# Pooled attention and a cosine router on one core: output columns in token order, stores of 128 contiguous rows, gates of the last rows by VectorE, a schedule with other step lengths

## The chip, the cores and the metric

The kernel runs on one core of a Trainium2 chip. The metric is the device time of one execution in microseconds; the time before is the median of three runs. Everything is computed in one launch.

## The reference

```python
def _attn_ref(q, k, v):                 # 8 batches, 8 heads, 576 tokens, 64 wide
    k_p = k.reshape(B, H, Sp, pool, D).mean(axis=3)      # pool = 8, Sp = 72
    v_p = v.reshape(B, H, Sp, pool, D).mean(axis=3)
    scores = scale * np.matmul(q, k_p.transpose(0, 1, 3, 2))
    attn = softmax(scores)
    return np.matmul(attn, v_p)
...
def _moe_ref(x, expert_emb, tau, w1, w2):   # x: 4608 tokens x 512, 8 experts, F = 1024
    logits = xn @ en.T / tau            # xn, en: rows of x and expert_emb, normalized
    expert_idx = np.argmax(logits, axis=1)
    gate_w = probs[np.arange(N), expert_idx]   # probs: softmax of logits
    for e in range(E):
        mask = expert_idx == e
        h = np.maximum(x[mask] @ w1[e], 0.0)
        out[mask] = gate_w[mask, None] * (h @ w2[e])
    return out
```

The rows of x are the attention's output, heads side by side, so a batch is 576 consecutive rows of the output, each of 512 floats (2 KB).

## The kernel before

The eight batches are worked through one after the other, and attention of batch b+1 stands among the expert products of batch b. All tokens of a batch are taken to go to one expert, chosen from the mean of its pooled v; a loop at the end (line 727 on) repairs batches where other experts are needed, and is left at once where there are none.

**Loads.** GpSimd's queue loads K, V and Q of a batch (576 KB each as fp16, cast on the way from float) and the chosen expert's weights W1 and W2 (1 MB each as fp16). A round for batch b is the list `PK, W1(b), K(b+1), Q(b+1), W2(b), V(b+2)` (line 229 on); `PK` (`pick`, line 266) reads the expert's number, which VectorE finds in `choose` (line 363) from the folded V of the same batch. So a round cannot be issued before that step.

**Attention.** VectorE halves K and V by adding (`halve`, line 300, and the folds, lines 304 and 312), transposes Q in blocks (`qT`, line 385) and copies the transposed K (`kpT`, line 402). Q is loaded with 18 consecutive tokens on each of 32 partitions a head (R = 32, T = 18). TensorE makes scores in two halves (`SC`, line 415), ScalarE the exponentials (`EX`, line 428), TensorE the products with V (`PV`, line 443), VectorE divides (line 453), TensorE transposes to `xt_all`, which has the 576 tokens of a batch as columns. In the kernel before, a column is t * 32 + p for the token p * 18 + t.

**Router.** Lines 489 to 531 make the gate of every token: `gate` (line 524) leaves it in `gm_all`, 128 rows by 5 chunks. The fifth chunk holds only 64 new tokens, in its rows 64 to 127. `NE` (line 539) copies their gates to rows 0 to 63 of `gl_all` by a DMA on SyncE's queue.

**Expert products.** `H` (eight steps, line 548) multiplies W1 with `xt_all`; `HE` (lines 557, 559) is the relu, on ScalarE or VectorE; `Y` (four steps, line 563) multiplies with W2 for 128 tokens each, `YE` (lines 575, 577) scales by the gate, `ST` (line 622) stores 256 KB. The last 64 tokens are one step `YL` (line 569), with the left half of the columns in rows 0 to 63 and the right half in rows 64 to 127. `YF` scales the left half on VectorE with `gl_all` (line 577, 64x256), `YG` the right half on ScalarE with `gm_all` (line 575, 64x256), and `SL` (`put_last`, line 644) stores the two halves, 64 KB each. All stores are issued on SyncE's queue. `Y` tiles come from a ring of six, PSUM tiles from a ring of four; a tile that `YL` wrote is free again when `YF` and `YG` have run.

**Order.** `Plan` lists every step with its engine, a length in us, a priority, and what it needs. `order` (line 76) goes through a clock of its own and always takes the step that can begin first; instructions of an engine stand in the program in that order, and an engine runs them in that order. So a length changes the places of steps, not the work.

Of the kernel before, what the change touches and what calls it, by code (L numbers as in the profile page):

```python
# [16 lines left out]
ALU = mybir.AluOpType  # L17
# [38 lines left out]
class Plan:  # L56
# [5 lines left out]
    def add(self, name, engines, busy, prio, run, after=(), takes=(), uses=(), late=0.0,  # L62
            mode=None):
        if isinstance(engines, str):
            engines = (engines,)
        if not isinstance(busy, tuple):
            busy = (busy,) * len(engines)
        s = Step(name, engines, busy, late, prio, [a for a in after if a], list(takes),
                 list(uses), run, mode)
        for b in s.takes + s.uses:  # L70
            b.left += 1
        self.steps.append(s)
        self.by_name[name] = s
        return name
# [68 lines left out]
def kernel(  # L143
# [83 lines left out]
    add = plan.add  # L227
# [44 lines left out]
    def attention(b, base):  # L272
        P = PERIOD
        kr, vr, qq = Buf(kr_r), Buf(vr_r), Buf(qq_r)
        qT, kp, kpT, vp = Buf(qT_r), Buf(kp_r), Buf(kpT_r), Buf(vp_r)
        n = lambda s, *i: s + str(b) + "".join(f".{j}" for j in i)

        def pr(f):
            return base + f * P
# [3 lines left out]
        if b == 0:  # L283
            for i in range(NQ):
                add(n("Q", i), 'POOL', 0.8, at_load(n("Q", i)), lambda i=i: load_q(b, qq, i, 1),
                    takes=[] if i else [qq], uses=[qq] if i else [], mode=1.43, late=0.9)
        else:
            add(n("Q", 0), 'POOL', 0.8, at_load(n("Q", 0)), lambda: load_q(b, qq, 0, NQ),
                takes=[qq], mode=2.85, late=0.9)
# [35 lines left out]
        if b == 0:  # L325
            pv_, pk_ = Buf(psum), Buf(psum)
            add(n("KA"), 'PE', 1.75, pr(-0.5), lambda: sums(kr, pk_), [n("K"), "PRE"],
                takes=[pk_], uses=[kr], late=0.22)
            add(n("KB"), 'ACT', 0.55, pr(-0.5), lambda: [nc.scalar.copy(
                out=kp_rows()[:, a],  # L330
                in_=by_group(pk_.tile[0:G, 0:512].rearrange("g (h d) -> g h d", d=D))[:, a])
                for a in range(NQ)], [n("KA")], takes=[kp], uses=[pk_], late=0.12)
            add(n("VA"), 'PE', 1.75, pr(-0.45), lambda: sums(vr, pv_), [n("V"), "PRE"],
                takes=[pv_], uses=[vr], late=0.22)
            add(n("VB"), 'DVE', 0.6, pr(-0.45), lambda: nc.vector.tensor_copy(
                out=vp_rows(), in_=pv_.tile[0:G, 0:512].rearrange("g (a c) -> g a c", a=HP)),
                [n("VA")], takes=[vp], uses=[pv_], late=0.12)
        else:
            add(n("VA"), 'DVE', 1.14, pr(-0.5), lambda: halve(vr.tile, 4), [n("V")], uses=[vr],
                late=0.1)  # L340
            add(n("VB"), 'DVE', 0.95, pr(-0.5), v_fold, [n("VA")], takes=[vp], uses=[vr],
                late=0.1)
            add(n("KA"), 'DVE', 1.14, pr(-0.2), lambda: halve(kr.tile, 4), [n("K")], uses=[kr],
                late=0.1)
            add(n("KB"), 'DVE', 1.0, pr(-0.2), k_fold, [n("KA")], takes=[kp], uses=[kr],
                late=0.1)


        pg = Buf(psum)
# [18 lines left out]
        def onehot():  # L368
# [5 lines left out]
        add(n("GC"), 'DVE', 0.1, pr(-0.5), lambda: nc.vector.tensor_copy(  # L374
            out=mv.tile, in_=pg.tile[:, 0:4]), [n("GM")], takes=[mv], uses=[pg], late=0.1)
        add(n("GL"), 'PE', 0.13, pr(-0.5), guess, [n("GC")], uses=[pg, mv], late=0.22)
        add(n("GD"), 'DVE', 0.35, pr(-0.5), choose, [n("GL")], uses=[pg], late=0.1)
        add(n("GE"), 'DVE', 0.2, pr(0.5), onehot, [n("GD")], late=0.1)


        for a in range(NQ):
            for i in range(2):
# [10 lines left out]
        def kt():  # L393
# [5 lines left out]
                        identity=ident_h[0:G, 0:G])  # L399

        add(n("KT"), 'PE', 0.14, pr(0.0), kt, [n("KB"), "PRE"], takes=[pk], uses=[kp], late=0.22)
        add(n("KE"), 'DVE', 0.25, pr(0.0), lambda: nc.vector.tensor_copy(  # L402
            out=kpT.tile.rearrange("p a c g -> p (a c g)"),
            in_=pk.tile.bitcast(FP16)[:, 0:2 * NQ * G]), [n("KT")], takes=[kpT], uses=[pk],
            late=0.1)

        at = [Buf(at_r) for _ in range(HP)]
        for half in range(2):
            for a in range(NQ):
                pair = [Buf(psum), Buf(psum)]  # L410

                def score(a=a, half=half, pair=pair):
                    for c in range(2):
                        for m in range(QG):
                            nc.tensor.matmul(  # L415
                                out=pair[m // 2].tile[0:G, m % 2 * 512:m % 2 * 512 + HALF],
                                lhsT=kpT.tile[ts(m, R), a, c, :],
                                rhs=qT.tile[ts(m, R), a, ts(half, T // 2), c, :],
                                start=(c == 0), stop=(c == 1))

                f = 0.02 + 0.2 * half + 0.1 * a
                add(n("SC", half, a), 'PE', 0.35, pr(f), score,
                    [n("KE"), n("QT", a, half)], takes=pair, uses=[qT, kpT], late=0.22,
                    mode='r32')
                for i in range(2):
                    t = at[2 * a + i]
                    add(n("EX", half, 2 * a + i), 'ACT', 0.56, pr(f),
                        lambda t=t, p=pair[i], half=half: nc.scalar.activation(  # L428
                            out=t.tile[:, :, ts(half, HALF)],
                            in_=p.tile[0:G].rearrange("g (r c) -> g r c", r=2)[:, :, 0:HALF],  # L430
                            func=AF.Exp, scale=escale),
                        [n("SC", half, a)], takes=[] if half else [t],
                        uses=[pair[i]] + ([t] if half else []), late=0.12)


        for c in range(NC):
            px, r, x, pt = Buf(psum), Buf(r_r), Buf(x_r), Buf(psum)
# [33 lines left out]
            def square(c=c, x=x):  # L471
# [3 lines left out]
            f = 0.5 + 0.08 * c  # L475
            add(n("PV", c), 'PE', 0.27, pr(f), pv,
                [n("EX", i, j) for i in range(1 if c < 2 else 2) for j in range(HP)] + [n("VB")],
                takes=[px], uses=at + [vp], late=0.22)
            add(n("XM", c), 'DVE', 0.84, pr(f), norm, [n("PV", c)], takes=[r, x], uses=[px],
                late=0.12)  # L480
            add(n("XT", c), 'PE', 0.23, pr(f), xtr, [n("XM", c)], takes=[pt], uses=[x], late=0.22)
            add(n("XE", c), 'DVE', 0.34 if c < 4 else 0.22, pr(f), xcopy, [n("XT", c)], uses=[pt],
                late=0.1)
# [15 lines left out]
        def pick_max():  # L499
# [8 lines left out]
            late=0.22)  # L508
# [15 lines left out]
        def gate():  # L524
            nc.vector.tensor_reduce(out=z, in_=lg, axis=AX.X, op=ALU.add)
            nc.vector.tensor_tensor(out=lg, in0=oh_all[:, b],
                                    in1=eb_all[:, b].unsqueeze(1).to_broadcast([128, NC, E]),
                                    op=ALU.mult)
            nc.vector.reciprocal(out=gate_all[:, b], in_=z)
            nc.vector.tensor_reduce(out=gm_all[:, b], in_=lg, axis=AX.X, op=ALU.add)  # L530
            nc.vector.tensor_tensor(out=gm_all[:, b], in0=gm_all[:, b], in1=gate_all[:, b],
                                    op=ALU.mult)

        add(n("NA"), 'POOL', 1.25, pr(1.3), root, [n("SQ", c) for c in range(NC)], late=0.1)
        add(n("NB"), 'DVE', 0.4, pr(1.3), scaled, [n("NA"), n("RE")], late=0.1)
        add(n("NC"), 'ACT', 0.25, pr(1.3), lambda: nc.scalar.activation(
            out=lg, in_=lg, func=AF.Exp, bias=lnxs), [n("NB")], late=0.1)
        add(n("ND"), 'DVE', 0.65, pr(1.35), gate, [n("NC"), n("GE")], late=0.1)
        add(n("NE"), 'SP', 0.1, pr(1.35), lambda: nc.sync.dma_start(
            out=gl_all[0:64, b:b + 1], in_=gm_all[64:128, b, 4:5]), [n("ND")], mode=0.1, late=1.0)  # L540

# [33 lines left out]
            nc.vector.tensor_scalar(out=dst, in0=src, scalar1=g, scalar2=None, op0=ALU.mult)  # L577

    def chunk_rows(o_b, c):
        return o_b.rearrange("(p t) d -> t p d", t=T)[4 * c:4 * c + 4]  # L580

    def last_rows(o_b):
        return o_b.rearrange("(p t) (r d) -> r t p d", t=T, r=2)[:, 16:18]

    def ffn(b, base):
        n = lambda s, *i: s + str(b) + "".join(f".{j}" for j in i)
# [43 lines left out]
        def last(r):  # L630
            rows = ts(r, 64)
            scale_rows(y.tile[rows, 0:DH], p.tile[rows, r * 512:r * 512 + DH],
                       g[rows, 4:5] if r else gl_all[:, b:b + 1], 'ACT' if r else 'DVE')

        add(n("YF"), 'DVE', 0.35, f - 2.0, lambda: last(0), [n("YL"), n("NE")], takes=[y],
            uses=[p], late=0.12)
        add(n("YG"), 'ACT', 0.38, f - 2.0, lambda: last(1), [n("YL"), n("ND")], uses=[p, y],
            late=0.12)
# [88 lines left out]
    with tc.For_i(0, n_val, 1) as i:  # L727
        f_val = nc.values_load(ext_i[0:1, ds(i, 1)], min_val=0, max_val=1)
        with tc.If(f_val > 0):
# [19 lines left out]
                h_mm(xt_c, w1, w, psum.tiles[w % 4])  # L749
                h_relu(psum.tiles[w % 4], hT[w], 'ACT' if w % 2 else 'DVE')  # L750
            gl = gl_all[:, B:B + 1]
            nc.sync.dma_start(out=gl, in_=gmx[64:128, 4:5])
            y, o = y_r.tiles[0], y_r.tiles[1]
            for c in range(5):
                p = psum.tiles[c % 4]
# [56 lines left out]
```

## Time and profile before

| | us |
|---|---|
| median of 3 runs | 284.74 (284.48 to 286.25) |
| the profiled execution's own time | 285.62 |
| its span, first to last instruction | 284.0 |
| TensorE busy with products | 205.8 |
| VectorE busy | 144.5 |
| ScalarE busy | 119.4 |
| GpSimd busy | 43.9 |

The profile shows one execution. Its span is shorter than its own time by what lies before the first and behind the last instruction. Busy times overlap each other. PE is TensorE, PEld its weight loads, DVE VectorE, ACT ScalarE, POOL GpSimd and SP SyncE; a q behind a name means its instruction queue, which issues DMAs. L548 is line 548 of the kernel before. A number in brackets behind a row is the idle time of the engine just before it and what ended it. A DMA share is the mean busy share of the core's sixteen DMA engines; packet times can overlap, so it can exceed 1.

### The profile page before, as it was taken

What the parts mean: (1) busy time and instruction counts of PE and PEld (TensorE: products, weight loads), DVE (VectorE), ACT (ScalarE), POOL (GpSimd) and SP (SyncE); (2) the same over time, 40 slices, a digit from 0 to 9 for tenths busy, and PEclk for the clock granted to TensorE, in tenths of its full rate; (3) what the DMA queues carried; (4) which work ended last, traced back from release to release, by engine and by line L of the source; (5) the groups of instructions that cost most, each with busy time, mean ns of one, the idle gap of its engine ahead of it and who ended that gap; (6) DMA issues with size and microseconds to landing.
All of it is one profiled execution on the core that took longest, in us unless ns stands there. A gap on an engine that the chain in (4) does not pass through costs nothing.

```text
span 284.0 us, 5224 instructions
## 1 busy us (share of the span) xinstructions
PE 205.8 (72%) x2006; PEld 128.9 (45%) x2007; DVE 144.5 (51%) x398; ACT 119.4 (42%) x239; POOL 43.9 (15%) x59
## 2 busy tenths in 40 slices
PE   2898798868995597938995698904997069899600
PEld 1566664544563353624563354602555036476300
DVE  2178677945791557724792458514495043550200
ACT  2046285374457153453447254620542056454400
POOL 7052400700160005100060004100021000010000
PEclk9999999997999599896999599975899658999955
DMA  5979999999999937995299937992149421121120
GB/s 70 196 122 202 206 208 208 222 227 227 194 184 230 180 76 140 222 216 115 67 173 221 187 79 139 212 203 81 60 82 217 96 88 48 38 82 51 47 103 21
DMA packets 29147, 40.76 MB, mean 144 GB/s; under 512 B 4536, under 2 KB 14776, under 8 KB 29120
## 3 DMA queue, kind: packets, MB, share of 16 engines
q0 software_dynamic: 23184, 30.95, 62.5%
q1 hardware_dynamic: 5936, 9.46, 10.0%
q8 instruction: 16, 0.26, 0.4%
q14 instruction: 11, 0.09, 0.1%
HBM read 61.88 MB, written 9.44 MB: 251 GB/s over the span
## 4 chain that ended last, share of the span: by engine, by line
DMA 64%; PE 21%; DVE 4%; issue 3%; POOL 1%; ACT 1%; POOLq 1%; DVEq 0%
DMA vr<-in_v_dram 27%; DMA kr<-in_k_dram 19%; DMA gl_all<-gm_all 18%; PE pa L548 11%; PE pa L563 6%; PE pa L415 2%; DVE y L577 2%; PE pa L569 1%; POOL w L256 1%; DVE vr L301 1%; PE pa L322 1%; DVE xt_all L466 0%; ACT hT L557 0%; DVE kr L301 0%; POOLq L267 0%
## 5 line engine op out<-in xcount | busy, mean ns | idle before, releaser
L548 PE MATMUL pa<-xt_all,w 128*128 128x288 f16 x512 | 80.2, 313 | 33.4 <-DVE y L577 31.2
L548 PEld LDWEIGHTS <-w 128*128 128x128 f16 x512 | 51.3, 105 | 56.8 <-issue 41.6
L563 PE MATMUL pa<-w,hT 128*128 128x512 f16 x256 | 60.8, 383 | 4.9 <-DVE y L577 2.4
L428 ACT ACTIVATE at<-pa 72x576 f16<-72x576 f32 x64 | 37.4, 641 | 35.2 <-PE pa L415 35.1
L557 ACT ACTIVATE hT<-pa 128x576 f16<-128x576 f32 x49 | 31.8, 650 | 37.0 <-PE pa L548 35.0
L563 PEld LDWEIGHTS <-hT 128*128 128x128 f16 x256 | 24.6, 98 | 30.9 <-issue 7.3
L575 ACT ACTIVATE y<-pa,gm_all 128x512 f32<-128x512 f32 (+1 forms) x32 | 20.0, 630 | 39.9 <-PE pa L563 25.5
L472 ACT ACTIVATE sq<-x 128x512 f16<-128x512 f16 x40 | 25.1, 628 | 22.8 <-DVE x L453 18.8
L256 POOL DMA_DIRECT2D w<-in_moe_w_dram x8 | 6.4, 804 | 152.9 <-PE pa L563 120.2
L301 DVE TENSOR_TENSOR vr<-vr 72x2048 f16<-72x2048 f16 (+1 forms) x14 | 13.4, 954 | 32.8 <-DMA vr<-in_v_dram 32.6
L453 DVE TENSOR_TENSOR x<-pa,r 128x512 f16<-128x512 f32 x40 | 27.7, 691 | 1.7
L415 PE MATMUL pa<-qT,kpT 32*72 32x288 f16 x256 | 16.5, 341 | 11.4 <-DVE ssq_all L520 11.2
L385 DVE STREAM_TRANSPOSE qT<-qq 128x576 f16<-128x576 f16 x32 | 23.3, 756 | 1.5 <-DMA qq<-in_q_dram 1.5
L559 DVE TENSOR_SCALAR hT<-pa 128x576 f16<-128x576 f32 x15 | 11.4, 757 | 24.7 <-PE pa L548 24.4
L516 POOL TENSOR_TENSOR ssq_all<-ssq_all,half_c 128x5 f32<-128x5 f32 x8 | 9.9, 1242 | 51.1 <-ACT sq L472 51.1
L577 DVE TENSOR_SCALAR y<-pa,gl_all 64x256 f32<-64x256 f32 x8 | 3.8, 473 | 27.4 <-DMA gl_all<-gm_all 14.3
L466 DVE COPY xt_all<-pa 128x512 f16<-128x512 f16 (+1 forms) x40 | 14.8, 383 | 2.5 <-PE pa L461 2.4
L461 PE MATMUL pa<-ident_h,x 128*128 128x128 f16 x160 | 14.4, 224 | 2.2 <-DVE x L453 2.0
L301 DVE TENSOR_TENSOR kr<-kr 72x2048 f16<-72x2048 f16 (+1 forms) x14 | 13.3, 947 | 5.2 <-DMA kr<-in_k_dram 5.1
L415 PEld LDWEIGHTS <-kpT 32*72 32x72 f16 x256 | 5.5, 118 | 21.0 <-DVE kpT L402 11.6
L461 PEld LDWEIGHTS <-x 128*128 128x128 f16 x160 | 11.0, 100 | 8.8 <-DVE x L453 3.6
L443 PE MATMUL pa<-vpx,at 72*128 72x65 f16 x320 | 14.5, 194 | 0.0
(87 smaller groups left out, 174.6 us busy)
## 6 DMA issues: line engine op xcount, KB each, us to landing
w<-in_moe_w_dram POOLq DMA_DIRECT2D x16, 1024.0 KB, 24.2
out_dram<-y SPq DMA_DIRECT2D x32, 256.0 KB
vr<-in_v_dram POOLq DMA_DIRECT2D x8, 576.0 KB, 35.3
kr<-in_k_dram POOLq DMA_DIRECT2D x8, 576.0 KB, 25.7
qq<-in_q_dram POOLq DMA_DIRECT2D x7, 576.0 KB, 32.0
out_dram<-y SPq DMA_DIRECT2D x16, 64.0 KB
qq<-in_q_dram POOLq DMA_DIRECT2D x2, 288.0 KB, 10.1
gl_all<-gm_all SPq DMA_DIRECT2D x8, 0.2 KB
```

The costliest lines, as they stand in the source:

```text
L301: nc.vector.tensor_tensor(out=t[:, :, 0:m], in0=t[:, :, 0:m], in1=t[:, :, m:2 * m], op=ALU.add)
L385: nc.vector.transpose(out=qT.tile[:, a].rearrange("p t c e -> p (t c e)")[:, cols], in_=qq.tile[:, a, cols]),
L415: nc.tensor.matmul(out=pair[m // 2].tile[0:G, m % 2 * 512:m % 2 * 512 + HALF], lhsT=kpT.tile[ts(m, R), a, c, :], rhs=qT.tile[ts(m, R), a, ...
L428: lambda t=t, p=pair[i], half=half: nc.scalar.activation(out=t.tile[:, :, ts(half, HALF)], in_=p.tile[0:G].rearrange("g (r c) -> g r c", r ...
L453: nc.vector.tensor_tensor(out=x.tile, in0=pxv[:, :, 1:129].rearrange("p a (r d) -> p a r d", d=D), in1=r.tile.rearrange("p (a r) -> p a r" ...
L461: nc.tensor.transpose(out=pt.tile.bitcast(FP16)[:, ts(w, 128)], in_=xf[:, ts(w, 128)], identity=ident_h)
L466: nc.vector.tensor_copy(out=xt_all[:, b, :, c * 128:c * 128 + 128 - o], in_=pt.tile.bitcast(FP16)[:, 0:512].rearrange("p (w t) -> p w t", ...
L472: nc.scalar.activation(out=sq, in_=x.tile.rearrange("p a r d -> p (a r d)"), func=AF.Square, accum_out=ssq_all[:, b, c:c + 1])
L548: nc.tensor.matmul(out=p[:, half * 512:half * 512 + HALF], lhsT=w1v[:, kk, w // 2, w % 2, :], rhs=xt[:, kk, ts(half, HALF)], start=(kk == ...
L557: nc.scalar.activation(out=dst, in_=src, func=AF.Relu)
L563: nc.tensor.matmul(out=p, lhsT=hT[w][:, ts(c, 128)], rhs=w2[:, w // 2, w % 2, :], start=(w == 0), stop=(w == 7))
L575: nc.scalar.activation(out=dst, in_=src, func=AF.Copy, scale=g)
```

## The change

Five things are edited.

The columns of `xt_all` become tokens in their natural order. A score half is now 16 of the 32 partitions' worth of tokens (columns t, p with 16 values of p) instead of 9 values of t, so the first half needs both transposes; the exponential reads its PSUM tile with the t and p extents exchanged, and writes token order.

With that, a chunk of 128 columns is 128 consecutive rows of the output, and `chunk_rows` and `last_rows` no longer pick rows 18 apart. The gates of the last 64 rows are multiplied a second time on VectorE, straight to rows 0 to 63 of `gl_all`, and the DMA step `NE` is gone; `YF` needs `ND` instead. Eight step lengths of the plan are other numbers. In the repair loop a DMA becomes a VectorE copy.

```diff
-            add(n("VB"), 'DVE', 0.95, pr(-0.5), v_fold, [n("VA")], takes=[vp], uses=[vr],
+            add(n("VB"), 'DVE', 1.0, pr(-0.5), v_fold, [n("VA")], takes=[vp], uses=[vr],
...
-                                rhs=qT.tile[ts(m, R), a, ts(half, T // 2), c, :],
+                                rhs=qT.tile[ts(m, R), a, :, c, ts(half, R // 2)],
...
-                add(n("SC", half, a), 'PE', 0.35, pr(f), score,
-                    [n("KE"), n("QT", a, half)], takes=pair, uses=[qT, kpT], late=0.22,
+                add(n("SC", half, a), 'PE', 0.27, pr(f), score,
+                    [n("KE"), n("QT", a, 0), n("QT", a, 1)], takes=pair, uses=[qT, kpT], late=0.22,
...
-                            out=t.tile[:, :, ts(half, HALF)],
-                            in_=p.tile[0:G].rearrange("g (r c) -> g r c", r=2)[:, :, 0:HALF],
+                            out=t.tile[:, :, ts(half, HALF)].rearrange(
+                                "g r (p t) -> g r p t", t=T),
+                            in_=p.tile[0:G].rearrange("g (r c) -> g r c", r=2)[:, :, 0:HALF]
+                            .rearrange("g r (t p) -> g r p t", t=T),
...
+            nc.vector.tensor_tensor(out=gl_all[:, b:b + 1], in0=gm_all[64:128, b, 4:5],
+                                    in1=gate_all[64:128, b, 4:5], op=ALU.mult)
...
-        add(n("NE"), 'SP', 0.1, pr(1.35), lambda: nc.sync.dma_start(
-            out=gl_all[0:64, b:b + 1], in_=gm_all[64:128, b, 4:5]), [n("ND")], mode=0.1, late=1.0)
...
     def chunk_rows(o_b, c):
-        return o_b.rearrange("(p t) d -> t p d", t=T)[4 * c:4 * c + 4]
+        return o_b[ts(c, 128)]
...
     def last_rows(o_b):
-        return o_b.rearrange("(p t) (r d) -> r t p d", t=T, r=2)[:, 16:18]
+        return o_b[S - 64:S].rearrange("p (r d) -> r p d", r=2)
...
-        add(n("YF"), 'DVE', 0.35, f - 2.0, lambda: last(0), [n("YL"), n("NE")], takes=[y],
+        add(n("YF"), 'DVE', 0.35, f - 2.0, lambda: last(0), [n("YL"), n("ND")], takes=[y],
...
-            nc.sync.dma_start(out=gl, in_=gmx[64:128, 4:5])
+            nc.vector.tensor_copy(out=gl, in_=gmx[64:128, 4:5])
```

The other lengths are those of KB, GD, GE, KE, NB and ND on VectorE (1.0 to 1.08, 0.35 to 0.42, 0.2 to 0.4, 0.25 to 0.2, 0.4 to 0.6, 0.65 to 0.8). Lines behind the first additions are 2 to 4 higher in the changed kernel.

First, SyncE's queue at the start of the program: the copy of `gl_all`, the five stores of batch 0, and the copy for batch 1. Before:

```order
L539 DMA gl_all<-gm_all 64x1
L622 DMA out_dram<-y_109 4x32x512
L622 DMA out_dram<-y_110 4x32x512
L622 DMA out_dram<-y_111 4x32x512
L622 DMA out_dram<-y_112 4x32x512
L644 DMA out_dram<-y_113 2x32x256 x2
L539 DMA gl_all<-gm_all 64x1
```

And in the changed kernel, from the first store on:

```order
L624 DMA out_dram<-y_109 128x512
L624 DMA out_dram<-y_110 128x512
L624 DMA out_dram<-y_111 128x512
L624 DMA out_dram<-y_112 128x512
L646 DMA out_dram<-y_113 64x256 x2
L624 DMA out_dram<-y_114 128x512
```

The small copies are gone, and the extents that a store has in the output, from the outside in, are 128 by 512 or 64 by 256 instead of 4 by 32 by 512 or 2 by 32 by 256.

Second, VectorE in the middle of the H products of one of the later batches: the fold of V for two batches on (`vr`, `vpx`), `YF` (`y`, `gl_all`), the gate step and relus (`hT`). Before:

```order
L301 TENSOR_TENSOR vr_74<-vr_74 72x8x256
L301 TENSOR_TENSOR vr_74<-vr_74 72x8x128
L315 TENSOR_TENSOR vpx_84<-vr_74 72x4x128
L577 TENSOR_SCALAR y_109<-pa_61,gl_all 64x256
L525 TENSOR_REDUCE lmax_all<-lg_all 128x5
L526 TENSOR_TENSOR lg_all<-oh_all,eb_all 128x40
L529 RECIPROCAL gate_all<-lmax_all 128x5
L530 TENSOR_REDUCE gm_all<-lg_all 128x5
L531 TENSOR_TENSOR gm_all<-gm_all,gate_all 128x5
L559 TENSOR_SCALAR hT_97<-pa_61 128x576
```

In the changed kernel:

```order
L301 TENSOR_TENSOR vr_74<-vr_74 72x8x256
L579 TENSOR_SCALAR y_109<-pa_64,gl_all 64x256
L561 TENSOR_SCALAR hT_107<-pa_62 128x576
L527 TENSOR_REDUCE lmax_all<-lg_all 128x5
L528 TENSOR_TENSOR lg_all<-oh_all,eb_all 128x40
L531 RECIPROCAL gate_all<-lmax_all 128x5
L532 TENSOR_REDUCE gm_all<-lg_all 128x5
L533 TENSOR_TENSOR gl_all<-gm_all,gate_all 64x1
L535 TENSOR_TENSOR gm_all<-gm_all,gate_all 128x5
L301 TENSOR_TENSOR vr_74<-vr_74 72x8x128
L315 TENSOR_TENSOR vpx_84<-vr_74 72x4x128
```

The first addition of the V fold, which waits for the V load, still stands ahead of `YF`; the rest of the fold went behind the gate step, a relu came forward, and the gate step has one multiply more.

Third, VectorE some rows earlier: the last transposes of Q (`qT`), the router's maxima (`lmax_all`, `oh_all`, `lg_all`) and the copy of the transposed K (`kpT`). Before:

```order
L385 STREAM_TRANSPOSE qT_77<-qq_75 128x576 x2
L503 TENSOR_REDUCE lmax_all<-pa_62 128x5
L504 TENSOR_TENSOR oh_all<-pa_62,lmax_all 128x40
L505 TENSOR_TENSOR lg_all<-pa_62,lmax_all 128x40
L385 STREAM_TRANSPOSE qT_77<-qq_75 128x576
L402 COPY kpT_81<-pa_64 128x288
```

In the changed kernel:

```order
L385 STREAM_TRANSPOSE qT_77<-qq_75 128x576 x2
L505 TENSOR_REDUCE lmax_all<-pa_62 128x5
L506 TENSOR_TENSOR oh_all<-pa_62,lmax_all 128x40
L507 TENSOR_TENSOR lg_all<-pa_62,lmax_all 128x40
L385 STREAM_TRANSPOSE qT_77<-qq_75 128x576
L402 COPY kpT_81<-pa_63 128x288
```

Nothing moved here: `kpT`, which every score product reads, is copied behind the last transpose in both.

## Rows read from the trace of the kernel before

**Rows 1.** Busy us of PE, PEld, DVE, ACT, POOL; granted clock; DMA share; GB/s.

```profile
0.00:32.27 32.27, 22.89 (x242) 15.90 (x244) 16.47 (x50) 10.67 (x24) 13.41 (x26) 1.00 0.95 155
32.27:56.61 24.34, 22.27 (x245) 14.20 (x244) 20.50 (x55) 13.32 (x27) 6.68 (x7) 1.00 1.16 212
56.61:83.70 27.09, 23.16 (x240) 14.38 (x237) 17.53 (x47) 15.11 (x30) 4.48 (x6) 0.94 1.08 208
83.70:117.48 33.78, 25.18 (x244) 15.34 (x241) 18.62 (x49) 14.37 (x29) 5.87 (x7) 0.85 0.85 166
117.48:147.94 30.46, 23.69 (x243) 14.68 (x240) 18.59 (x49) 13.92 (x28) 4.48 (x6) 0.89 0.75 149
147.94:179.09 31.15, 24.17 (x243) 14.65 (x240) 17.24 (x48) 15.01 (x30) 4.35 (x6) 0.89 0.82 162
179.09:215.38 36.29, 24.30 (x244) 14.91 (x240) 18.98 (x50) 13.92 (x28) 2.75 (x4) 0.81 0.64 130
215.38:251.46 36.08, 24.01 (x235) 14.62 (x232) 12.86 (x37) 14.07 (x28) 1.85 (x2) 0.81 0.35 87
251.46:269.53 18.07, 16.15 (x119) 10.19 (x115) 3.70 (x20) 8.97 (x15) 0.00 (x0) 1.00 0.18 58
269.53:284.00 14.47, 0.00 (x0) 0.00 (x0) 0.00 (x0) 0.00 (x0) 0.00 (x0) 0.51 0.17 63
```

**Rows 2.** Waits of PE: us in total, times, longest.

```profile
PE pa L548 <- DVE y L577: 31.2, 5, 11.1
PE pa L415 <- DVE ssq_all L520: 11.2, 1, 11.2
```

**Rows 3.** Timeline of PE around its wait at 184 us: start, length, instructions.

```profile
179.09 1.14 PE L548 MATMUL pa<-xt_all,w 128*128 128x288 f16 x8
...
195.67 2.08 PE L548 MATMUL pa<-xt_all,w 128*128 128x288 f16 x8 [11.10 <-DVE y L577]
```

**Rows 4.** Timeline of DVE at its last three long waits.

```profile
190.33 1.94 DVE L301 TENSOR_TENSOR vr<-vr 72x2048 f16<-72x2048 f16 x2 [8.65 <-DMA vr<-in_v_dram]
...
195.15 0.48 DVE L577 TENSOR_SCALAR y<-pa,gl_all 64x256 f32<-64x256 f32 x1 [2.42 <-DMA gl_all<-gm_all]
...
228.76 0.48 DVE L577 TENSOR_SCALAR y<-pa,gl_all 64x256 f32<-64x256 f32 x1 [11.91 <-DMA gl_all<-gm_all]
```

**Rows 5.** Timeline of POOL: the issue of the last V load.

```profile
144.61 0.86 POOL L245 DMA_DIRECT2D vr<-in_v_dram  x1
```

**Rows 6.** Timeline of SP's queue: two copies of gl_all.

```profile
172.95 7.50 SPq L539 DMA_DIRECT2D gl_all<-gm_all  x1
...
199.65 16.35 SPq L539 DMA_DIRECT2D gl_all<-gm_all  x1
```

**Rows 7.** DMA queues on the page: packets, MB, share of 16 engines' span.

```profile
q0 software_dynamic: 23184, 30.95, 62.5%
q1 hardware_dynamic: 5936, 9.46, 10.0%
```

**Rows 8.** Windows: one with a V load outstanding, two with stores alone.

```profile
163.50:171.50 8.00, 7.52 (x74) 4.58 (x74) 4.26 (x12) 3.83 (x8) 0.00 (x0) 0.96 0.32 76
...
273.00:276.00 3.00, 0.00 (x0) 0.00 (x0) 0.00 (x0) 0.00 (x0) 0.00 (x0) 0.50 0.29 109
277.00:279.00 2.00, 0.00 (x0) 0.00 (x0) 0.00 (x0) 0.00 (x0) 0.00 (x0) 0.50 0.14 49
```

**Rows 9.** Groups by line and form: busy us, mean ns, idle us before them.

```profile
L428 ACT ACTIVATE at<-pa 72x576 f16<-72x576 f32 x64 | 37.4, 641 | 35.2 <-PE pa L415 35.1
...
L575 ACT ACTIVATE y<-pa,gm_all 128x512 f32<-128x512 f32 x24 | 16.2, 684 | 25.5 <-PE pa L563 25.5
...
L575 ACT ACTIVATE y<-pa,gm_all 64x256 f32<-64x256 f32 x8 | 3.7, 468 | 14.5 <-DVE y L577 14.0 <-DMA out_dram<-y 0.4
...
L531 DVE TENSOR_TENSOR gm_all<-gm_all,gate_all 128x5 f32<-128x5 f32 x8 | 1.3, 165 | 0.3
```

**Rows 10.** Instructions of the repair loop's head: ns, first and last start.

```profile
L727 SPq EVENT_SEMAPHORE  x21: 17/28/28, 274.5 to 282.0; - x21
```

More of the change, by code (lines that the diff above doesn't have):

```diff
@@ L344, in attention @@
                 late=0.1)
-            add(n("KB"), 'DVE', 1.0, pr(-0.2), k_fold, [n("KA")], takes=[kp], uses=[kr],
+            add(n("KB"), 'DVE', 1.08, pr(-0.2), k_fold, [n("KA")], takes=[kp], uses=[kr],
                 late=0.1)
@@ L376, in attention @@
         add(n("GL"), 'PE', 0.13, pr(-0.5), guess, [n("GC")], uses=[pg, mv], late=0.22)
-        add(n("GD"), 'DVE', 0.35, pr(-0.5), choose, [n("GL")], uses=[pg], late=0.1)
-        add(n("GE"), 'DVE', 0.2, pr(0.5), onehot, [n("GD")], late=0.1)
+        add(n("GD"), 'DVE', 0.42, pr(-0.5), choose, [n("GL")], uses=[pg], late=0.1)
+        add(n("GE"), 'DVE', 0.4, pr(0.5), onehot, [n("GD")], late=0.1)
         for a in range(NQ):
@@ L401, in attention @@
         add(n("KT"), 'PE', 0.14, pr(0.0), kt, [n("KB"), "PRE"], takes=[pk], uses=[kp], late=0.22)
-        add(n("KE"), 'DVE', 0.25, pr(0.0), lambda: nc.vector.tensor_copy(
+        add(n("KE"), 'DVE', 0.2, pr(0.0), lambda: nc.vector.tensor_copy(
             out=kpT.tile.rearrange("p a c g -> p (a c g)"),
@@ L534, in attention @@
         add(n("NA"), 'POOL', 1.25, pr(1.3), root, [n("SQ", c) for c in range(NC)], late=0.1)
-        add(n("NB"), 'DVE', 0.4, pr(1.3), scaled, [n("NA"), n("RE")], late=0.1)
+        add(n("NB"), 'DVE', 0.6, pr(1.3), scaled, [n("NA"), n("RE")], late=0.1)
         add(n("NC"), 'ACT', 0.25, pr(1.3), lambda: nc.scalar.activation(
             out=lg, in_=lg, func=AF.Exp, bias=lnxs), [n("NB")], late=0.1)
-        add(n("ND"), 'DVE', 0.65, pr(1.35), gate, [n("NC"), n("GE")], late=0.1)
-        add(n("NE"), 'SP', 0.1, pr(1.35), lambda: nc.sync.dma_start(
-            out=gl_all[0:64, b:b + 1], in_=gm_all[64:128, b, 4:5]), [n("ND")], mode=0.1, late=1.0)
+        add(n("ND"), 'DVE', 0.8, pr(1.35), gate, [n("NC"), n("GE")], late=0.1)
     def h_mm(xt, w1, w, p):
```

## The prediction

> **What bounds the kernel now.** I began with one table: the busy time of each engine between the first relu product of one batch and that of the next, cut at 32.27, 56.61, 83.70, 117.48, 147.94, 179.09, 215.38 and 251.46 us [rows 1]. [...] VectorE (12.9 to 20.5 us) and ScalarE (13.3 to 15.1 us) are never full. The last stretch has no busy engine at all: 14.47 us after the last VectorE instruction, with DMA at 0.17.
>
> Next, who makes TensorE wait. Two groups hold 42.4 us: 31.2 us in front of the H products, five times, and 11.2 us once in front of a score product [rows 2]. The names there are releasers, VectorE instructions that were late themselves. [...]
>
> VectorE runs in program order, and at these places it stands in front of one of two DMAs [rows 4]: at 190.33 us the V rows arrive after 8.65 us of waiting, at 195.15 us gl_all after 2.42 more, and at 228.76 us gl_all alone after 11.91 us. Behind each stands YF, the scaling of the last 64 rows, which frees the PSUM tile that TensorE needs. The V load that ended the first wait was issued at 144.61 us [rows 5]: 45.7 us for 0.6 MB. The gl_all copy is 256 bytes, yet its issue on SyncE's queue took 7.50 us at 172.95 us and 16.35 us at 199.65 us [rows 6], behind output stores that back up in the same queue.
>
> Why are a late V and a slow gl_all the same fault? Loads (queue 0) use 62.5% of sixteen DMA engines' time over the span and stores (queue 1) 10.0% [rows 7]. Where nothing but stores moves, the DMA share stops at 0.29 with 109 GB/s, then at 0.14 with 49 GB/s, though SyncE's queue has plenty left [rows 8]. Sixteen times these are 4.6 and 2.2 engines. The store of four t values has an outermost extent of 4 in DRAM, that of the last rows 2. So I read that a store is dealt out over 4 engines, or 2. Then 10.0% x 284.0 x 16 / 8 = 56.8 engine-us of stores a batch fall on four engines, 14.2 us on each, on top of 62.5% x 284.0 / 8 = 22.2 us of loads. These four need 36.4 us of packet time a batch, the other twelve 22.2. Packet times overlap (the share reaches 1.16), so divided by that: 31.4 us, close to the periods measured, where the twelve need 19.1. The window at 163.50 us fits: a V load is outstanding, and only 0.32 of the DMA engines work [rows 8].
>
> [...]
>
> **The change part by part.** *Stores.* 32 stores of 256 KB and 16 of 64 KB keep size and run length, but their DRAM side is now 128 (or 64) rows from the outside in. The loads, with 72 or 128 outermost, reach shares of 1.16. If stores go over all sixteen engines, each engine has 22.2 + 3.5 = 25.7 us of packet time a batch, 22.2 us by the same overlap. [...] The V load then comes a whole round earlier than VectorE asks for it. From below (stores stay on four engines) this part gives nothing; I take the full effect, since every load of that outer extent shows it, and removal of the V waits.
>
> *gl_all.* Eight DMAs leave SyncE's queue; eight VectorE multiplies of 64x1 enter the gate step, in front of the 128x5 multiply of 165 ns [rows 9]: 8 x 0.17 = 1.3 us on an engine that idles a third of a period, so nothing. If that cover were gone it costs those 1.3 us. The waits of 2.42 and 11.91 us for it go whatever the stores do. What is late next at these places is the V fold, which still stands in front of YF in most batches.
>
> Both together take away the two groups of rows 2: 31.2 + 11.2 = 42.4 us. With the waits goes the low clock: TensorE's busy time beyond 22.27 us in the six periods is 0.89 + 2.91 + 1.42 + 1.90 + 2.03 + 1.74 = 10.9 us [rows 1].
>
> *End.* 14.47 us pass after the last VectorE instruction [rows 1]; SyncE goes through the closing code from 274.5 to 282.0 us [rows 10], waiting for stores that still move at 277 to 279 us [rows 8]. With stores four times as wide I take 6 us, between 4 (the closing code alone) and 14.5: a gain of 8.5.
>
> *Columns in token order.* A score product now reads 18 runs of 16 columns where it read 9 runs of 32, and needs both transposes of its group. I take nothing for that: before and after, the copy of kpT that every score product needs stands behind all four transposes on VectorE, so no score product could start ahead of them. The exponential reads its PSUM tile with a stride of 16 elements and writes it packed. No row shows ScalarE with a strided PSUM read. From below: 0, as 288 elements stay 288. From above, by the slope of two scalings, (684 - 468) ns / 256 = 0.84 ns an element, a second pass over 576 elements is 0.49 us on 641 ns [rows 9], x 64 = 31 us of ScalarE. I take 0, nearest to the row of the same operation and size, and keep 31 us of ScalarE, of which the path would see a part.
>
> [...]
>
> *Step lengths.* They reorder steps within a batch: at the place of the long wait YF, a relu and the gate step now come ahead of the second half of the V fold, though still behind its first. That is worth about a microsecond where V is late and nothing where it is not; I take nothing, since I expect V in time.
>
> **Sum.** Against the profiled execution: 284.0 - 42.4 - 10.9 - 8.5 = 222.2 us of span; its own time was 285.62, 1.6 more, hence 223.8; the median of 284.74 lies 0.9 lower, so 223 us. A second route: 32.27 of start, 24.34, six periods of 23.2 (36.29 less the 11.1 of idling in it and 2.0 of clock; 36.08 less 11.2 and 1.7 is the same), 18.07, 6 and 1.6 make 221.5.
>
> **Rivals.** *The DMA engines become the bound.* For: without overlap of packets a round is 25.7 us, above the 23.2 of TensorE. Against: the first period ran at share 1.16. Price: five periods fed by a V load, 5 x 2.5 = 12.5 us, 235 us. Chance 0.14.
>
> *The strided exponential is slow.* 3.9 us more of ScalarE a batch, on 15 of 23. For: relus and exponentials alternate there while TensorE waits for PSUM tiles. Against: ScalarE has the room. At 1.5 us of it exposed in 8 batches: 235 us; all of it exposed 254. Chance 0.12. [...]
>
> *The stores gain nothing from their shape* (slow for another reason, as writing HBM). Against: 0.29 and 0.14 stand as 4 to 2. Then only the waits for gl_all go, 2.4 + 11.2 us, and the clock loss of the last period, 1.7: 269 us. Chance 0.05.
>
> *Slower.* The exponential on ScalarE, if strided reads cost it several passes: to bring seven periods back to 32 us ScalarE must be full, 17 us more for eight exponentials, 2.1 us each, so more than four extra passes of 0.49. At five: 15.1 + 8 x 2.43 = 34.5 us a batch, and 32.3 + 7 x 34.5 + 18.1 + 8 = 300 us. Nothing in the trace comes near that. Chance 0.02. No change within 1% (about what a measurement of this kernel can tell): 0.01.
>
> **How the numbers follow.** The forecast has 0.66. Its own range is 211 (periods of TensorE's 22.27 alone, a tail of 4 us, a start 2 us shorter) to 231 (periods of 24.4). Two rivals lie at 235, so the range runs to 242 and leaves out 2 in 10: both at once, 269 and above, and less than 211. Faster: 0.66 + 0.14 + 0.12 + 0.05 = 0.97.
>
> **What would show it.** Right: no wait of TensorE above 1 us in front of H or score products, a granted clock near 1.00 up to the last product, periods of 22.5 to 24.5 us, stores issued in about 0.5 us each with a DMA share above 0.5 where they alone move, less than 7 us behind the last VectorE instruction, the exponential at 0.64 us. Wrong: V waits of several us on VectorE with the DMA share above 1 (first rival), the exponential above 0.8 us (second), or stores that still hold SyncE's queue for several us each (third).

## The result, and the profile after

The changed kernel takes 220.88 us (median of 4 runs, 220.55 to 221.29) where the kernel before took 285.5 in the same comparison: a ratio of 0.7731, 95% interval 0.7683 to 0.7779. A second measurement of the same kernel gave 220.8 us and 0.7701 (0.7672 to 0.7729). The forecast was 223 us, in a range of 211 to 242. The measurements named e3, e7 and e9 below hold one slower run each, which is in their medians and left out of their ratios.

The windows cut at the first H product of each batch, as in [rows 1]; columns are the length, then busy us of PE, PEld, DVE, ACT, POOL, granted clock, DMA share, GB/s.

```profile
0.00:32.20 32.20, 22.37 (x245) 15.83 (x247) 16.38 (x50) 10.84 (x24) 13.42 (x26) 1.00 0.96 155
32.20:56.57 24.37, 23.68 (x245) 15.03 (x244) 18.46 (x52) 14.79 (x30) 5.67 (x7) 0.93 1.15 217
56.57:80.08 23.51, 22.13 (x241) 14.05 (x240) 18.31 (x50) 14.22 (x29) 6.19 (x7) 1.00 1.16 228
80.08:102.78 22.70, 21.79 (x237) 13.84 (x236) 18.87 (x52) 14.21 (x29) 4.69 (x6) 1.00 1.15 230
102.78:125.76 22.98, 22.02 (x247) 14.25 (x245) 17.89 (x48) 14.49 (x29) 5.51 (x7) 1.00 1.14 227
125.76:150.31 24.55, 22.22 (x244) 14.18 (x242) 18.79 (x51) 13.89 (x28) 4.49 (x6) 1.00 1.14 223
150.31:173.31 23.00, 21.89 (x244) 14.06 (x241) 18.69 (x51) 14.37 (x29) 2.73 (x3) 1.00 1.00 199
173.31:196.00 22.69, 21.52 (x231) 13.78 (x228) 14.25 (x40) 12.74 (x26) 1.16 (x1) 1.00 0.56 136
196.00:214.00 18.00, 16.14 (x119) 10.19 (x115) 3.79 (x21) 8.99 (x15) 0.00 (x0) 1.00 0.22 78
214.00:219.70 5.70, 0.00 (x0) 0.00 (x0) 0.07 (x1) 0.00 (x0) 0.00 (x0) 0.77 0.10 24
```

The start, the first period and the last product stretch are as long as they were, although the clock of the first period is now 0.93. The six periods between went from 27 to 36 us each to 22.69 to 24.55, and in all six the clock is 1.00. The DMA share stays at 1.14 to 1.16 through the first period and the next four, where it had fallen from 1.16 to between 0.75 and 1.08; it ends at 1.00 and 0.56 as the loads run out. Behind the last VectorE instruction 5.70 us are left of 14.47.

No DMA moves from 200 to 209 us; after that only the stores of the last batch do. Two windows of that time, to be read beside [rows 8]:

```profile
209.00:210.00 1.00, 1.00 (x6) 0.49 (x5) 0.00 (x0) 0.00 (x0) 0.00 (x0) 1.00 0.98 365
213.00:214.00 1.00, 0.00 (x0) 0.00 (x0) 0.86 (x6) 0.00 (x0) 0.00 (x0) 1.00 1.00 361
```

Stores alone now reach a DMA share of 0.98 to 1.00 and 361 to 365 GB/s, where they stopped at 0.29 and 109 GB/s.

TensorE's waits, the rows that answer to [rows 2] (us in total, times, longest):

```profile
PE pa L497 <- DVE xt_all L468: 2.0, 1, 2.0
PE pa L550 <- DVE lg_all L507: 1.3, 4, 0.5
PE pa L415 <- ACT y L577: 1.2, 1, 1.2
PE pa L550 <- ACT hT L559: 1.1, 3, 0.4
...
PE pa L550 <- DVE y L579: 0.2, 1, 0.2
```

Nothing in front of an H or score product is longer than 1.2 us; the two groups of 31.2 and 11.2 us are gone. VectorE's waits for loads:

```profile
DVE vr L301 <- DMA vr<-in_v_dram: 5.0, 4, 1.6
...
DVE kr L301 <- DMA kr<-in_k_dram: 3.8, 3, 2.3
```

A wait for V is at most 1.6 us, where the one in [rows 4] was 8.65. SyncE's stores (ns, least, median and most of one issue; first and last start), before and after:

```profile
L622 SPq DMA_DIRECT2D out_dram<-y x32: 528/582/7648, 47.1 to 267.8; - x32
L644 SPq DMA_DIRECT2D out_dram<-y x16: 523/2295/6815, 65.1 to 269.0; - x16
...
L624 SPq DMA_DIRECT2D out_dram<-y x32: 332/335/368, 46.3 to 212.2; - x32
L646 SPq DMA_DIRECT2D out_dram<-y x16: 472/510/1354, 56.2 to 213.2; - x16
```

The longest issue of a store fell from 7.65 us to 1.35. The queues on the page, as in [rows 7], and two groups by line, as in [rows 9]:

```profile
q0 software_dynamic: 23184, 30.95, 80.6%
q1 hardware_dynamic: 5904, 9.46, 13.0%
```

```profile
L428 ACT ACTIVATE at<-pa 72x576 f16<-72x576 f32 x64 | 37.5, 640 | 3.9 <-PE pa L415 3.9
...
L533 DVE TENSOR_TENSOR gl_all<-gm_all,gate_all 64x1 f32<-64x1 f32 x8 | 1.2, 155 | 0.3
```

The exponential that reads with a stride takes 640 ns, after 641 without. The new multiply takes 155 ns.

### The profile page after: what moved, and what is told of

Same layout as the page of the kernel before. It is cut to its first block, busy times and chain, and to the rows that moved or that the text cites. A ratio compares the mean times of both kernels' runs of the same rounds, so it can differ in the third digit from the quotient of the medians.

```text
span 219.7 us, 5197 instructions
## 1 busy us (share of the span) xinstructions
PE 193.8 (88%) x2009; PEld 125.2 (57%) x2010; DVE 145.5 (66%) x407; ACT 118.5 (54%) x238; POOL 43.9 (20%) x59
## 3 DMA queue, kind: packets, MB, share of 16 engines
q1 hardware_dynamic: 5904, 9.46, 13.0%
## 4 chain that ended last, share of the span: by engine, by line
PE 45%; DMA 34%; DVE 10%; issue 3%; ACT 3%; POOL 1%; POOLq 1%; DVEq 0%; ACTq 0%
PE pa L550 20%; DMA kr<-in_k_dram 20%; PE pa L565 19%; DMA vr<-in_v_dram 14%; PE pa L415 3%; DVE qT L385 3%; ACT y L577 2%; DVE y L579 2%; PE pa L445 1%; DVE kr L301 1%; DVE xt_all L468 1%; DVE x L455 1%; PE pa L571 1%; PE pa L322 1%; POOL w L256 1%
## 5 line engine op out<-in xcount | busy, mean ns | idle before, releaser
L550 PE MATMUL pa<-xt_all,w 128*128 128x288 f16 x512 | 70.0, 290 | 2.6 <-DVE lg_all L507 1.3
L565 PE MATMUL pa<-w,hT 128*128 128x512 f16 x256 | 59.9, 378 | 3.6 <-ACT y L577 2.0
L550 PEld LDWEIGHTS <-w 128*128 128x128 f16 x512 | 48.7, 99 | 19.6 <-issue 7.8
L559 ACT ACTIVATE hT<-pa 128x576 f16<-128x576 f32 x47 | 30.6, 651 | 34.9 <-PE pa L550 31.0
L474 ACT ACTIVATE sq<-x 128x512 f16<-128x512 f16 x40 | 25.2, 629 | 23.2 <-DVE x L455 20.5
L577 ACT ACTIVATE y<-pa,gm_all 128x512 f32<-128x512 f32 (+1 forms) x33 | 20.6, 633 | 19.4 <-PE pa L565 13.8
L561 DVE TENSOR_SCALAR hT<-pa 128x576 f16<-128x576 f32 x17 | 12.8, 753 | 12.5 <-PE pa L550 12.5
L415 PE MATMUL pa<-qT,kpT 32*72 32x288 f16 x256 | 14.5, 294 | 1.6 <-ACT y L577 1.2
L445 PE MATMUL pa<-vpx,at 72*128 72x65 f16 x320 | 15.1, 194 | 0.0
L463 PEld LDWEIGHTS <-x 128*128 128x128 f16 x160 | 10.5, 97 | 7.5 <-DVE x L455 2.8
L653 PE MATMUL pa<-ones_m 128*128 128x256 f16 x92 | 13.8, 297 | 0.8 <-ACT at L428 0.7
L445 PEld LDWEIGHTS <-at 72*128 72x128 f16 x320 | 12.9, 98 | 2.0 <-issue 1.1
```

What stands on the lines that cost most here:

```text
L415: nc.tensor.matmul(out=pair[m // 2].tile[0:G, m % 2 * 512:m % 2 * 512 + HALF], lhsT=kpT.tile[ts(m, R), a, c, :], rhs=qT.tile[ts(m, R), a, ...
L445: nc.tensor.matmul(out=px.tile[:, o:o + 65], lhsT=at[h // 2].tile[:, h % 2, c0:c0 + 128], rhs=vp.tile[:, h // 2, 1 + h % 2 * 65:66 + h % 2 ...
L463: nc.tensor.transpose(out=pt.tile.bitcast(FP16)[:, ts(w, 128)], in_=xf[:, ts(w, 128)], identity=ident_h)
L474: nc.scalar.activation(out=sq, in_=x.tile.rearrange("p a r d -> p (a r d)"), func=AF.Square, accum_out=ssq_all[:, b, c:c + 1])
L550: nc.tensor.matmul(out=p[:, half * 512:half * 512 + HALF], lhsT=w1v[:, kk, w // 2, w % 2, :], rhs=xt[:, kk, ts(half, HALF)], start=(kk == ...
L559: nc.scalar.activation(out=dst, in_=src, func=AF.Relu)
```

## The experiments

Theory 1: the outermost extent of a store in the output sets over how many DMA engines it is dealt out, four and two before, as [rows 8] were read, and these few engines held up the loads as well; that carries the gain. Theory 2: the gl_all copies in SyncE's queue carry it. Theory 3: the stores were slow because their rows lay apart in the output. Beside them, the step lengths were to be weighed, and what bounds the kernel now.

### Gates by VectorE alone (e2_gl_by_vector_alone)

```diff
+            nc.vector.tensor_tensor(out=gl_all[:, b:b + 1], in0=gm_all[64:128, b, 4:5],
+                                    in1=gate_all[64:128, b, 4:5], op=ALU.mult)
...
-        add(n("NE"), 'SP', 0.1, pr(1.35), lambda: nc.sync.dma_start(
-            out=gl_all[0:64, b:b + 1], in_=gm_all[64:128, b, 4:5]), [n("ND")], mode=0.1, late=1.0)
...
-        add(n("YF"), 'DVE', 0.35, f - 2.0, lambda: last(0), [n("YL"), n("NE")], takes=[y],
+        add(n("YF"), 'DVE', 0.35, f - 2.0, lambda: last(0), [n("YL"), n("ND")], takes=[y],
```

> The kernel before with one part of the change: the gates of the last rows by VectorE, no gl_all DMA. Stores, columns and step lengths as before. Theory 1 (the spread of the stores over DMA engines carries most of the gain): V still comes late, only the waits for gl_all and the clock loss behind one of them go, 264 to 274 us. Theory 2 (the gl_all DMA in SyncE's queue carries it): below 235 us.

Measured: 274.2 us, ratio to the kernel before 0.9641 (0.9583 to 0.9699), 0.2 us above the slow edge of what theory 1 gave and 39 us above the bound of theory 2. VectorE's waits, the first line that of the kernel before:

```profile
DVE vr L301 <- DMA vr<-in_v_dram: 32.6, 7, 8.7
...
DVE vr L301 <- DMA vr<-in_v_dram: 37.9, 7, 8.1
...
DVE y L577 <- DMA out_dram<-y: 3.0, 2, 1.9
```

The wait for gl_all is gone and the waits for V have grown from 32.6 to 37.9 us; a new one, for a store to release its tile, has come. So the copy alone was worth 285.09 - 274.2 = 10.9 us, where the whole change brings 285.5 - 220.88 = 64.6. Part of its wait seems to have passed to the next load, which is argued from these sums.

### Consecutive rows, dealt out over 4 or 2 (e4_rows_together_outer_4)

```diff
-        return o_b[ts(c, 128)]
+        return o_b[ts(c, 128)].rearrange("(p a) d -> a p d", a=4)
...
-        return o_b[S - 64:S].rearrange("p (r d) -> r p d", r=2)
+        return o_b[S - 64:S].rearrange("(p a) (r d) -> r a p d", r=2, a=2)
```

> The changed kernel, but each store deals its 128 consecutive rows out with an outermost extent of 4 (the last rows: 2), so rows land in other places of the same 256 KB; nothing else differs. Theory 1 (the outermost extent sets how many DMA engines a store gets): 258 to 275 us, DMA share about 0.25 where stores alone move, V waits back on VectorE. Theory 3 (stores were slow because their rows lie 18 apart in DRAM): within 2 us of the changed kernel, 219 to 223.

Measured: 275.2 us, ratio 0.9662 (0.9617 to 0.9706), 0.2 us above the upper end for theory 1 and 52 above that for theory 3. The rows of a store fill one block of 256 KB, as in the changed kernel, though in the order of the store's extents they now lie 4 apart; and the time is that of rows 18 apart without the gl_all copies (274.2). The stretch after the last VectorE instruction (257.7 us), where only stores move, then the issues of stores:

```profile
259.00:263.00 4.00, 0.00 (x0) 0.00 (x0) 0.00 (x0) 0.00 (x0) 0.00 (x0) 0.52 0.28 107
```

```profile
L624 SPq DMA_DIRECT2D out_dram<-y x32: 536/1044/10527, 44.4 to 256.0; - x32
L646 SPq DMA_DIRECT2D out_dram<-y x16: 536/2818/8967, 54.8 to 257.3; - x16
```

```profile
DVE vr L301 <- DMA vr<-in_v_dram: 29.3, 7, 8.0
```

DMA share and rate of the stores alone (0.28, 107 GB/s) are those of [rows 8] (0.29, 109 GB/s), a single issue takes up to 10.5 us again, and the V waits are back. Theory 3 falls.

### The old rows, dealt out over 32 (e5_rows_apart_outer_32)

```diff
-        return o_b.rearrange("(p t) d -> t p d", t=T)[4 * c:4 * c + 4]
+        return o_b.rearrange("(p t) d -> p t d", t=T)[:, 4 * c:4 * c + 4]
...
-        return o_b.rearrange("(p t) (r d) -> r t p d", t=T, r=2)[:, 16:18]
+        return o_b.rearrange("(p t) (r d) -> r p t d", t=T, r=2)[:, :, 16:18]
```

> The kernel before, each store writing the same output rows as before (groups 18 apart) with the extents exchanged: 32 outermost, 4 inside, so rows land in other places; gl_all by DMA and step lengths as before. Theory 1: 220 to 232 us, with this one edit. Theory 3 (rows far apart): 278 to 290 us.

Measured: 222.33 us, ratio 0.7807 (0.7770 to 0.7844). This is the kernel before, with its columns, its gl_all DMA and its step lengths; two lines of it exchange the order of two extents. They bring 285.09 - 222.33 = 62.8 us, nearly all of the change. VectorE's wait for V, and two of the eight gl_all copies on SyncE's queue:

```profile
DVE vr L301 <- DMA vr<-in_v_dram: 4.9, 3, 2.6
...
39.92 0.56 SPq L539 DMA_DIRECT2D gl_all<-gm_all  x1
...
158.26 0.55 SPq L539 DMA_DIRECT2D gl_all<-gm_all  x1
```

Every issue of a copy takes 0.50 to 0.56 us, where [rows 6] had 7.50 and 16.35: with the stores spread, nothing backs up in front of it. The exchange does one thing more: four rows that follow one another in a store's extents are now neighbours in the output, so e4 and e5 by themselves don't part the number of engines from the nearness of rows. The next run does.

### Eight engines (e6_rows_together_outer_8)

```diff
-        return o_b[ts(c, 128)]
+        return o_b[ts(c, 128)].rearrange("(p a) d -> a p d", a=8)
...
-        return o_b[S - 64:S].rearrange("p (r d) -> r p d", r=2)
+        return o_b[S - 64:S].rearrange("(p a) (r d) -> r a p d", r=2, a=8)
```

> The changed kernel with 8 as the outermost extent of every store (rows land in other places of the same block). Theory 1, by engine time a batch: loads 22.2 us on each engine plus 56.8/8 = 7.1 us of stores on eight of them, 29.3 / 1.16 = 25.3 us a batch against 23.2: 226 to 238 us. Theory 3: 219 to 223 us.

Measured: 237.18 us, ratio 0.8339 (0.8287 to 0.8390). It lies between, and near the upper end of the range. In the order of the store's extents its rows lie 8 apart, farther than in e4, and it is 38 us faster: the nearness of rows is not what counts.

```profile
DVE vr L301 <- DMA vr<-in_v_dram: 17.2, 5, 7.3
...
L624 SPq DMA_DIRECT2D out_dram<-y x32: 603/603/733, 44.4 to 225.9; - x32
```

A stretch behind the last VectorE instruction, where only stores move, and the queue on the page:

```profile
228.00:231.00 3.00, 0.00 (x0) 0.00 (x0) 0.00 (x0) 0.00 (x0) 0.00 (x0) 0.68 0.48 171
```

```profile
q1 hardware_dynamic: 5520, 9.46, 12.7%
```

With an outermost extent of 4, 8 and 128 the V waits are 29.3, 17.2 and 5.0 us in total, the time is 275.2, 237.2 and 220.9 us, and the DMA share of stores alone is 0.28, 0.48 and 0.98 to 1.00. A store of 256 KB issues in 0.60 us here, at most 0.73, so SyncE's queue is not what is left; late loads are. That they are late on the eight engines that they share with the stores is inferred, since the trace has no row for a single DMA engine.

### gl_all by a DMA again (e1_gl_by_dma)

```diff
-            nc.vector.tensor_tensor(out=gl_all[:, b:b + 1], in0=gm_all[64:128, b, 4:5],
-                                    in1=gate_all[64:128, b, 4:5], op=ALU.mult)
...
+        add(n("NE"), 'SP', 0.1, pr(1.35), lambda: nc.sync.dma_start(
+            out=gl_all[0:64, b:b + 1], in_=gm_all[64:128, b, 4:5]), [n("ND")], mode=0.1, late=1.0)
...
-        add(n("YF"), 'DVE', 0.35, f - 2.0, lambda: last(0), [n("YL"), n("ND")], takes=[y],
+        add(n("YF"), 'DVE', 0.35, f - 2.0, lambda: last(0), [n("YL"), n("NE")], takes=[y],
```

> The changed kernel with gl_all copied by a DMA on SyncE's queue again. Theory 1: SyncE's queue is no longer backed up, the copy lands long before the last rows are scaled, 219 to 224 us. Theory 2 (the gl_all DMA was a cost of its own): 235 us or more.

Measured: 222.51 us, ratio 0.7798 (0.7750 to 0.7845). That is 1.6 to 1.7 us above the two measurements of the changed kernel; the interval lies above that of the second (to 0.7729) and overlaps that of the first (to 0.7779). So whether the copies cost anything is not shown, and it is nothing like the 13.6 us of [rows 2, 4] that were booked on them.

### The old step lengths (e3_old_lengths)

The changed kernel with the eight lengths of before; two of them:

```diff
-                add(n("SC", half, a), 'PE', 0.27, pr(f), score,
+                add(n("SC", half, a), 'PE', 0.35, pr(f), score,
...
-        add(n("ND"), 'DVE', 0.8, pr(1.35), gate, [n("NC"), n("GE")], late=0.1)
+        add(n("ND"), 'DVE', 0.65, pr(1.35), gate, [n("NC"), n("GE")], late=0.1)
```

> The changed kernel with the eight step lengths of before, so the order of before as far as the new dependencies let it. If the order is worth nothing, as forecast: 219 to 223 us. Rival: the new order carries part of the gain, 224 us or more.

Measured: 222.38 us, ratio 0.7756 (0.7712 to 0.7801), which overlaps both intervals of the changed kernel (0.7683 to 0.7779 and 0.7672 to 0.7729). By the ratios the new order is worth 0.7 or 1.6 us; that it is worth anything is not shown. What the order does can be seen in the profile, in VectorE's wait for V and TensorE's wait for `YF`:

```profile
DVE vr L301 <- DMA vr<-in_v_dram: 7.9, 3, 4.9
...
PE pa L550 <- DVE y L579: 5.0, 5, 3.6
```

TensorE waits 5.0 us for `YF` here (4.0 in e5, which has the old order too) and 0.2 us with the new order, where a part of the V fold stands behind `YF`. So the order can matter where V is late, as the prediction said; with the stores spread, V is seldom late.

### V ahead of W2 (e7_v_before_w2)

```diff
-        loads += [f"W2{b}"]
         if b + 2 < B:
             loads += [f"V{b + 2}"]
+        loads += [f"W2{b}"]
```

> The changed kernel with the V load of a round issued ahead of W2 instead of behind it. If the waits for V that are left on VectorE (5.0 us in four) reach TensorE: 217 to 220 us. If they are covered: 220 to 222 us; if W2 becomes late at the first Y product: 223 us or more.

Measured: 220.88 us, ratio 0.7707 (0.7667 to 0.7748): the same as the changed kernel. VectorE's waits for loads:

```profile
DVE kr L301 <- DMA kr<-in_k_dram: 6.7, 4, 3.0
...
DVE vr L301 <- DMA vr<-in_v_dram: 1.3, 1, 1.3
```

The wait for V shrinks from 5.0 to 1.3 us, and the wait for K grows from 3.8 to 6.7: the next load in the line is late instead.

### Few stores (e8_few_stores), with the changed kernel beside it (e9_changed_again)

```diff
-                out=chunk_rows(o_b, c), in_=y.tile), [n("YE", c)], uses=[y], mode=0.8, late=0.9)
+                out=chunk_rows(o_b, c), in_=y.tile) if b == B - 1 else None, [n("YE", c)], uses=[y], mode=0.8, late=0.9)
...
-        add(n("SL"), 'SP', 0.1, f, lambda: put_last(o_b, y.tile),
+        add(n("SL"), 'SP', 0.1, f, lambda: put_last(o_b, y.tile) if b == B - 1 else None,
```

> The changed kernel without the stores of the first seven batches (their output rows are not written), everything else in place. If the DMA engines are now a second bound beside TensorE: the waits for K and V on VectorE shrink and the time falls to 212 to 217 us. If TensorE alone bounds it: 218 to 222 us, with the DMA share well below that of the changed kernel.

> The changed kernel again, unaltered, as a yardstick on the same chip: 219 to 223 us.

Measured: 217.92 us, ratio 0.7614 (0.7587 to 0.7641), and 220.8 us for the changed kernel on the same chip. The expectation left a gap between 217 and 218, and the result fell into it. VectorE's waits for loads without the stores:

```profile
DVE qT L385 <- DMA qq<-in_q_dram: 2.1, 1, 2.1
...
DVE vr L301 <- DMA vr<-in_v_dram: 1.1, 2, 0.8
DVE kr L301 <- DMA kr<-in_k_dram: 0.8, 1, 0.8
```

Those for V and K go from 8.8 us to 1.9, and 2.9 us of the time with them. The gain is in few places. From one batch's first H product to the next, the periods are 24.38, 23.49, 22.70, 22.97, 24.58, 23.00 and 22.69 us in e9 and 23.31, 22.43, 22.70, 22.98, 23.00, 22.99 and 22.70 us without the stores. The first period of e9 and of e8:

```profile
31.88:56.26 24.38, 23.70 (x245) 14.93 (x244) 18.46 (x52) 14.79 (x30) 5.65 (x7) 0.93 1.15 217
...
32.89:56.20 23.31, 22.14 (x245) 14.25 (x244) 18.63 (x52) 14.68 (x30) 5.65 (x7) 1.00 1.16 209
```

The first difference is thus TensorE's clock, 1.56 us of its busy time, and two further periods hold the rest; in four of seven the stores cost nothing. Beside the loads, the stores of seven batches cost 2.9 us or less. What the loads alone cost was not tried: they all still run here.

## Why the prediction was right, point by point

**Which engines the stores use.** The step that carried the forecast, 0.29 and 0.14 of sixteen engines read as 4 and 2, is borne out by e4, e5 and e6: with outermost extents of 4, 8, 32 and 128 the time was 275.2, 237.2, 222.3 and 220.9 us, and it went with the extent in both directions, whatever rows were written. Sixteen times the DMA share of stores alone is 4.5 in e4, 7.7 in e6 and 15.7 to 16 in the changed kernel, for extents of 4, 8 and 128. That four become sixteen was the author's estimate in the forecast; the share of 0.98 to 1.00 is what shows it. There is another sign, which [rows 7] already held and the prediction did not use: the packets of queue 1. The 48 stores are 32 x 128 + 16 x 64 = 5120 runs. By the author's estimate of one packet a run, one more for each engine that a store uses, and 16 for the load of expert_emb, the rows come out exactly: 5120 + 16 + 48 x 16 = 5904 after, 5120 + 16 + 48 x 8 = 5520 in e6, and 5120 + 16 + 32 x 4 + 16 x 2 = 5296 with four and two in e2 and e4, to which the eight gl_all copies add 8 x (64 + 16) = 640, the 5936 of the kernel before. With sixteen engines and the copies it gives 6544, the count of e5. No view shows the kinds of packets; that the split fits all these runs is what speaks for it.

**What the waits were worth.** The forecast was that 42.4 us of TensorE's waits go. On the page the two lines had 33.4 and 11.4 us of idle time before; H and score products have 2.6 and 1.6 us now, 40.6 us less. One sign is missed by a little: the longest wait is 1.2 us and not below 1. *V and gl_all as one fault*: right, and more than the price of the third rival said. The waits for gl_all were booked there at 15.3 us with their clock loss, 269 us for a kernel that loses only them; e2 measured 274.2, and the V waits grew by 5.3 us when that cover was gone.

*V a whole round early*: this did not come. VectorE still waits for V four times, 5.0 us in all, and e7, where 1.3 us of it are left and K is late instead, takes the same time.

**The clock.** The forecast was 10.9 us. Eight H products took 2.08 us behind the wait of 11.10 us and 1.14 us ahead of it [rows 3]; at 1.00, in each of the six periods now, they take 1.14 to 1.16 us. TensorE's busy time in the six periods sums to 131.57 us, where [rows 1] sum to 144.51: 12.9 us, 2.1 of them because the periods now lie a little below the 22.27 us that the forecast took as the floor. Against it stand 1.4 us lost in the first period, at 0.93, where [rows 1] have 1.00.

**The end.** It takes 5.70 us, where 6 were forecast, and stores alone reach a share of 0.98 to 1.00, where more than 0.5 was named as a sign.

**The sum.** The span fell by 64.3 us, where 61.8 were forecast. The waits gave 1.8 us less than their term; TensorE's busy time over the whole span fell by 12.1 us, 1.2 more than the clock's term, and the end gave 0.3 more. The rest, 2.9 us of smaller waits, was in no term. So some 1.8 us of the closeness is luck, since a term that was too high met others that were too low.

**The edits costed at nothing.** The strided exponential takes 640 ns against 641, so the second rival and the slower one fall. Eight score matmuls, whose runs went from 32 to 16 columns, take 0.44 us at full clock before and after. The second multiply takes 8 x 155 ns = 1.2 us, where 1.3 were forecast; that it is hidden fits e1, which lacks it and is not faster. The step lengths were put at nothing, and e3 gives 0.7 or 1.6 us, not clear of the noise.

**What is late next.** The V fold was named, and the first rival priced DMA as the bound at 235 us, from 25.7 us of packet time a batch without overlap. The share of 1.14 to 1.16 over four periods shows that packets go on overlapping. That rival's excess over TensorE, 2.5 us a batch, is less than the stores' 3.5 of those 25.7, so a run without stores should gain all of its 12.5 us; e8 gains 2.9. The second route's period of 23.2 us holds: the six periods average 23.24, one of them, at 24.55, just above the 22.5 to 24.5 that was named as a sign.

## What to carry to other kernels

Look at the outermost extent of a store in DRAM before its size. With 4 there, the share of 0.29 was read as four of sixteen DMA engines for 256 KB, and loads on another queue, of other data, came late: VectorE waited up to 8.7 us for one load of V, 32.6 us in seven waits. When a wait for a tiny DMA stands in the profile, look for what stands in front of it in its queue: the issue of a gl_all copy fell from as much as 16.35 us to at most 0.56 when only the stores were changed (e5). When only one kind of transfer moves, compare its DMA share with its extents: here 0.28, 0.48 and 0.98 to 1.00 for 4, 8 and 128. A late transfer cost a second time here where TensorE idled for it, since the clock was low behind the wait (2.08 us for eight H products, 1.14 ahead of it): 40.6 us of waits went, and 12.9 us of slow products with them.

## What the runs showed of the hardware that was not expected

The time of issue of a store on SyncE's queue differs with its shape where nothing backs up: 335 ns (median) for 128 x 512, 603 ns for 8 x 16 x 512 in e6, 550 ns for 32 x 4 x 512 in e5. The number of extents alone does not set it, since 64 x 256 takes 510 ns.

The order of the extents mattered and the distance of the rows did not: 275.2 us with rows 4 apart in one block (e4) against 274.2 us with rows 18 apart (e2), both with outermost extents of four and two and without the copies.

In the changed kernel the clock fell in the first period behind a wait of 2.0 us at 30 us, and eight H products took 1.63 us; in the kernel before, which shows a wait of 1.9 us at the same place, they took 1.14 us and the period shows 1.00. The length of that wait alone does not settle it: the clock fell behind it in e9 and e5 too, at 1.77 and 1.7 us, and did not in e2 at 1.9. What tips it there was not tried.
